# v with two adjacent keys to a partition, multiplied in 64x64 tiles; logits in the PSUM banks of the q and k transposes

## The chip, the core and the metric

The kernel runs on one NeuronCore of a Trainium2 chip. The metric is the time of one execution on the device in microseconds (us); the time before is the median of three runs. All arithmetic that the change touches is in fp32.

## The reference, cut to what matters

Chunked attention, then two layers of experts. The change lies in the attention, and only there:

```python
# q, k, v: (B, H, S, D) = (8, 8, 576, 64); chunks of 64 keys, nc = 9
scores = (q_c @ k_c^T) / 8            # per batch, head, chunk: 64 x 64
attn = exp(scores - max) ; attn = attn / (sum(attn) + 1e-9)
out = attn @ v_c                      # 64 x 64
x = out.transpose(0, 2, 1, 3).reshape(4608, 512)
# then: logits = x @ w_gate, a greedy assignment of tokens to 8 experts,
# two layers per expert, and a maximum over three products before the last one
```

## The kernel before, in words

**The work.** There are 72 chunks (8 batches of 9), 8 heads in each. A *group* g is two chunks, all heads: 128 tokens. `G` = 36 groups; a *unit* u is four groups (8 chunks), `NU` = 9 units. The fifth unit (`ORDER[4]` is None) collects the odd chunk of each of the 8 batches.

**Loads.** `load_qk` (L52) brings half of a unit's heads of q or k in one DMA of 512 KB: 128 partitions, four adjacent rows (1 KB) to a partition; in the fifth unit it is one DMA of 128 KB per chunk into 16 partitions. `load_v` (L65) is called four times per unit (`part` 0 to 3), and each call issues two DMAs of 128 KB, one on SP's queue and one on POOL's (both on SP's for unit 0; in the fifth unit four of 64 KB). A key is a partition: head 2·part lies in partitions 0 to 63 and head 2·part+1 in 64 to 127, in runs of 256 bytes. The halves that are never written are zeros from a memset (L91, L92), so that one matmul over 128 partitions gives two heads side by side. `VB` has three buffers.

**The loop over groups (L245 to L292)** is a software pipeline written out by hand; each engine takes its instructions in this order. In turn i: a small DMA `tick` (L249) that holds SP's queue back until group i-1's maxima are there; the loads of the next units; `scores(i)` (16 matmuls of 64x64, two for each pair of heads and each chunk, into the two banks of pS); `scale(i-2)` and the DMA that writes x; `smax(i)`; `att_t(i-1)`, four transposes of the exponentials into pA, and `att_c`, their copy; then `trans`/`evac` of a piece of q and of k of the next unit (transposes into one of two pT banks, copied out in halves by ACT and DVE); `ssub(i)`, `expo(i)`; `x_t(i-2)` (transposes into pY); `pv(i-1)`; the logits; `x_c(i-2)`.

**pv (L175)** issues 8 matmuls per group: 128 partitions deep, 64 columns of weights, 128 columns moving; the two chunks c go to the two halves of the 64-column tiles.

**The logits** of a finished unit are computed in two steps in a PSUM bank of their own, pL: `logit1` (L206, four matmuls in 32-column tiles, then a copy `ls` on ACT) in the turns with i mod 4 = 2, behind `pv`, and `logit2` (L223, four transposes and a reduce on DVE) in the turns with i mod 4 = 3, behind `pv` too.

**evac (L117)** of k stores the keys in their natural order: key 4i+2w+r of a chunk, where the transposes deliver r by halves of the partitions, w by transposes and i along the row.

```python
dst = QT[nm, u][s * 64:s * 64 + 64, h0:h0 + 2].rearrange("p a j (i w r) -> p a (j i) w r", w=2, r=2)[:, :, :, :, r]
```

**After the loop** (L294 to L315) the last groups and logits drain; then come routing and the experts, which wait for all logits and for x.

Of the kernel before, what the change touches and what calls it, by code (L numbers as in the profile page):

```python
# [28 lines left out]
def attention(ctx, tc, q, k, v, wg_in, xd, L, ident, consts, early, tick, mark):  # L29
# [35 lines left out]
    def load_v(u, part):  # L65

        t = VB[u % 3]
        if ORDER[u] is not None:
            b, c = chunk(u, 0)
            for s in range(2):  # L70
                (nc.gpsimd if u and s else nc.sync).dma_start(
                    t[s * 64:(s + 1) * 64, :, part, s, :],
                    bass.AP(tensor=v.tensor, offset=v.offset + (b * H + 2 * part + s) * S * D + c * 64 * D,
                            ap=[[D, 64], [64 * D, 8], [1, D]]))
            return
        for j in (2 * part, 2 * part + 1):
            b, c = chunk(u, j)
            for s in range(2):
                (nc.gpsimd if u and s else nc.sync).dma_start(
                    t[s * 64:(s + 1) * 64, j, :, s, :],  # L80
                    bass.AP(tensor=v.tensor, offset=v.offset + b * H * S * D + s * S * D + c * 64 * D,
                            ap=[[D, 64], [2 * S * D, 4], [1, D]]))

# [21 lines left out]
    def trans(nm, u, n, bank="pT"):  # L105

        mark(nm + "T")
        if n == 0:
            QT[nm, u] = P.tile([128, 4, 8, 64], F32, name=nm + "T")
        pt = PS.tile([128, 2, 2, 128], F32, name=bank, bufs=2 if bank == "pT" else 1)  # L110
        PT[nm, u, n] = pt
        for a in range(2):
            for w in range(2):
                h = 4 * (n // 2) + 2 * a + n % 2
                nc.tensor.transpose(pt[:, a, w, :], QK[nm, u][:, h, w * 128:w * 128 + 128], ident)  # L115

    def evac(nm, u, n, r, eng):  # L117
        mark(nm + "E")
        s, h0 = n % 2, 2 * (n // 2)
        src = PT[nm, u, n][r * 64:r * 64 + 64].rearrange("p a w t -> p a t w")  # L120
        dst = QT[nm, u][s * 64:s * 64 + 64, h0:h0 + 2].rearrange("p a j (i w r) -> p a (j i) w r", w=2, r=2)[:, :, :, :, r]
# [24 lines left out]
    def expo(g):  # L146
        mark("exp")
        e = P.tile([128, 8, 64], F32, name="A")
        nc.scalar.activation(e, A[g], AF.Exp, scale=0.125)
        A[g] = e  # L150

    def sums(g, st):
        mark("sums")
        if st == 0:
            R[g] = P.tile([128, 8], F32, name="sm")
            nc.vector.tensor_reduce(R[g], A[g], op=OP.add, axis=AX.X)
        elif st == 1:
            nc.vector.tensor_scalar(R[g], R[g], 1e-9, None, op0=OP.add)
        else:
            r = P.tile([128, 8], F32, name="rc")  # L160
            nc.vector.reciprocal(r, R[g])
            R[g] = r

    def att_t(g):
        mark("attT")
        PA[g] = PS.tile([128, 4, 128], F32, name="pA", bufs=1)
        for hp in range(4):
            nc.tensor.transpose(PA[g][:, hp, :], A[g][:, 2 * hp:2 * hp + 2, :], ident)  # L168

# [5 lines left out]
    def pv(g):  # L175
        mark("pv")
        u, h = divmod(g, 4)
        PX[g] = PS.tile([128, 4, 128], F32, name="pX", bufs=1)
        for hp in range(4):
            for c in range(2):  # L180
                nc.tensor.matmul(PX[g][c * 64:(c + 1) * 64, hp, :], AT[g][:, hp, c * 64:c * 64 + 64],  # L181
                                 VB[u % 3][:, 2 * h + c, hp].rearrange("p s i -> p (s i)"),
                                 start=True, stop=True)

    def scale(g):
        mark("scale")
        X[g] = P.tile([128, 8, 64], F32, name="x", bufs=3)
        nc.vector.tensor_tensor(X[g], PX[g].rearrange("p a (s i) -> p (a s) i", s=2),
                                R[g][:, :, None].to_broadcast([128, 8, 64]), op=OP.mult)
        nc.gpsimd.dma_start(xd[tokens(g) * 128:(tokens(g) + 1) * 128, :], X[g].rearrange("p h d -> p (h d)"))  # L190
# [25 lines left out]
    def logit(j, w):  # L216
        mark("logit")
        pl = PS.tile([128, 4, 128], F32, name="pT")
        for dc in range(4):
# [3 lines left out]
    def logit2(j, w0=0, w1=4):  # L223
        mark("logit2")
        pl = PS.tile([128, 4, 4, 32], F32, name="pL", bufs=1)
        for w in range(w0, w1):
# [5 lines left out]

    banks = iter(("pT", "pT", "pX", "pY", "pL", "pA", "pT", "pT"))
    for n in (0, 2):
# [76 lines left out]
    for st in (1, 2, 3):  # L311
        early(0, st)
    logit(8, 2)
    logit2(8, 0, 2)
    logit(8, 3)  # L315


# [977 lines left out]
```

## Time and profile before

| | before |
|---|---|
| median of three runs | 1206.3 us (1203.97 to 1208.42) |
| the profiled execution: its time, its span | 1207.02 us, 1205.2 us |
| PE busy | 1172.5 us (97%) |
| DVE busy | 830.5 us (69%) |
| ACT busy | 412.7 us (34%) |
| POOL busy | 317.9 us (26%) |
| mean granted TensorE clock | 0.988 of full speed |
| DMA over the span | 242.99 MB, mean 202 GB/s |
| DMA packets under 512 B, under 2 KB | 30048, 101216 |

The busy shares are means over stages with different limits; the attention takes the first 166 us or so, and there ACT and DVE are far busier than over the whole (the windows below). An fp32 matmul shows as two records on PE, so the 8 matmuls of `pv` are x16 in the trace and the 16 of `scores` are x32; transposes are one record each. A row's us is from the start of its first instruction to the end of its last; since matmuls overlap, what a group of them takes of PE is read from the start of one group to the start of the next.

### The profile page before, as it was taken

The numbers are of one execution on the slowest core, as the hardware profiler recorded it, in microseconds if no ns is written. First come the engines' busy times: TensorE is split into PE (matmuls) and PEld (weight loads), VectorE is DVE, ScalarE is ACT, GpSimd is POOL, SyncE is SP. The second block draws the span as 40 slices with busy tenths as digits, with TensorE's granted clock in tenths as the row PEclk, the third lists the DMA queues.
The fourth block names the chain that finished last, engine by engine and source line by source line (L and its number), as shares of the span: only waits on it lengthen the run. The fifth ranks groups of instructions, "written<-read, shape, count | busy, mean of one in ns | idle before, by whom it ended". The sixth has DMA issues, their size and how long they took to land.

```text
span 1205.2 us, 23575 instructions
## 1 busy us (share of the span) xinstructions
PE 1172.5 (97%) x9508; PEld 1097.6 (91%) x9508; DVE 830.5 (69%) x1660; ACT 412.7 (34%) x674; POOL 317.9 (26%) x507
## 2 busy tenths in 40 slices
PE   7999978999999999999999999999999999999998
PEld 6788856989999999989999998998998998998996
DVE  6888976788898888888843565565565565664661
ACT  5888823232333333325423113113113113113111
POOL 8433201010337463766770002002002002002002
PEclk9999989999999999999999999999999999999999
DMA  9999516264566565559834773773773763773651
GB/s 264 256 271 269 162 45 184 66 233 150 177 193 209 184 215 183 186 192 283 281 144 162 274 259 123 276 260 119 280 259 118 281 259 115 285 258 114 235 189 53
DMA packets 138828, 242.99 MB, mean 202 GB/s; under 512 B 30048, under 2 KB 101216, under 8 KB 131808
## 3 DMA queue, kind: packets, MB, share of 16 engines
q1 hardware_dynamic: 118608, 180.90, 45.9%
q0 software_dynamic: 14976, 51.13, 12.7%
q10 hardware_dynamic: 5136, 9.46, 2.1%
q8 instruction: 75, 1.23, 0.4%
q14 instruction: 33, 0.27, 0.1%
HBM read 195.05 MB, written 46.40 MB: 200 GB/s over the span
## 4 chain that ended last, share of the span: by engine, by line
PE 53%; issue 35%; DMA 4%; DVE 3%; POOL 2%; ACT 1%; POOLq 1%; SPq 1%; ACTq 0%; DVEq 0%
PE acc L1105 17%; PE acc L1050 16%; DMA vb<-in_v_dram 3%; PE pX L181 2%; PE py L1143 2%; POOL out_dram L1227 2%; PE pT L115 2%; PE po L1219 2%; PE px L1143 2%; PE pz L1143 2%; PE pS L132 1%; PE pA L168 1%; PE pxt L821 1%; PE pY L199 1%; PE rp L553 1%
## 5 line engine op out<-in xcount | busy, mean ns | idle before, releaser
L1050 PE MATMUL acc<-xhi,chunk 128*128 128x288 f32 (+2 forms) x1024 | 207.4, 302 | 2.7 <-DVE hlo L1083 2.3
L1105 PE MATMUL acc<-hhi,chunk 128*128 128x288 f32 x1024 | 209.9, 299 | 0.0
L1227 POOL DMA_INDIRECT out_dram<-ot,ia x36 | 36.3, 1008 | 519.4 <-ACT ot L1225 518.8
L1050 PEld LDWEIGHTS acc<-xhi,chunk 128*128 128x128 f32 x1024 | 161.9, 189 | 3.8 <-DVE hlo L1083 2.7
L1105 PEld LDWEIGHTS acc<-hhi,chunk 128*128 128x128 f32 x1024 | 163.0, 188 | 0.3
L1105 PE MATMUL acc<-hlo,chunk 128*128 128x288 f32 x512 | 150.9, 295 | 0.0
L1219 PE MATMUL po<-chunk,h 128*128 128x512 f32 x648 | 149.3, 390 | 0.0
L1219 PEld LDWEIGHTS po<-chunk,h 128*128 128x128 f32 x648 | 121.5, 188 | 24.8
L1050 PE MATMUL acc<-xlo,chunk 128*128 128x288 f32 (+2 forms) x512 | 143.9, 296 | 0.0
L1143 PE MATMUL px<-xb,wa 128*128 128x384 f32 x648 | 130.0, 335 | 0.7 <-ACT ys L1112 0.7
L1143 PE MATMUL py<-xt,wb 128*128 128x384 f32 x648 | 129.9, 335 | 0.0
L1143 PEld LDWEIGHTS px<-xb,wa 128*128 128x128 f32 x648 | 113.9, 188 | 1.4 <-ACT ys L1112 1.0
L1143 PEld LDWEIGHTS py<-xt,wb 128*128 128x128 f32 x648 | 114.0, 188 | 0.5
L1164 ACT CAST h<-best 128x384 fp32r<-128x384 f32 x72 | 37.0, 513 | 198.1 <-DVE best L1162 121.3
L1105 PEld LDWEIGHTS acc<-hlo,chunk 128*128 128x128 f32 x512 | 96.2, 188 | 0.0
L1050 PEld LDWEIGHTS acc<-xlo,chunk 128*128 128x128 f32 x512 | 94.1, 189 | 0.0
L768 DVE TENSOR_TENSOR chunk<-raw,chunk 128x1024 fp32r<-128x1024 f32 x67 | 84.8, 1271 | 6.5 <-ACT chunk L761 5.7
L1074 ACT ACTIVATE hhi<-acc 128x576 fp32r<-128x576 f32 (+1 forms) x66 | 41.8, 637 | 137.2 <-PE acc L1050 135.3
L798 POOL DMA_INDIRECT xg<-xd,idx x40 | 43.3, 1082 | 169.2 <-DVE ohe L688 89.7
L1179 ACT COPY tmp<-px 128x384 f32<-128x384 f32 x54 | 25.8, 478 | 146.3 <-PE px L1143 146.3
L761 ACT CAST chunk<-raw 128x1024 fp32r<-128x1024 f32 x67 | 69.7, 1047 | 7.8 <-ACT ys L1112 6.4
L1083 DVE SCALAR_TENSOR_TENSOR hlo<-acc,hhi 128x576 fp32r<-128x576 f32 (+1 forms) x66 | 48.2, 735 | 30.9 <-ACT hhi L1074 30.5
(222 smaller groups left out, 2058.5 us busy)
## 6 DMA issues: line engine op xcount, KB each, us to landing
wb<-wdb SPq DMA_DIRECT2D x54, 1024.0 KB
wa<-wda SPq DMA_DIRECT2D x54, 768.0 KB
raw<-in_moe_w_dram SPq DMA_DIRECT2D x64, 512.0 KB
xd<-x POOLq DMA_DIRECT2D x36, 256.0 KB, 4.8
yd<-ys ACTq DMA_DIRECT2D x32, 288.0 KB
wdb<-pair POOLq DMA_DIRECT2D x18, 512.0 KB, 4.7
yraw<-yd SPq DMA_DIRECT2D x12, 768.0 KB
ink<-in_k_dram SPq DMA_DIRECT2D x16, 512.0 KB
```

The source lines that it names most:

```text
L761: nc.scalar.copy(hi, raw)
L768: nc.vector.tensor_tensor(lo, raw, hi.bitcast(F32), op=OP.subtract)
L798: nc.gpsimd.indirect_dma_start(out=g, out_offset=None, in_=xd[:, :], in_offset=bass.IndirectOffsetOnAxis(ap=rt.idx[r][:, t:t + 1], axis=0))
L1050: nc.tensor.matmul(acc[:, hf, :tk.stop - tk.start], w[a][:, dc, o:o + 128], x[:, dc, tk], start=n == 0, stop=n == 11)
L1074: nc.scalar.activation(hv, src, AF.Relu)
L1083: nc.vector.scalar_tensor_tensor(lv, src, 0.0, hv.bitcast(F32), op0=OP.max, op1=OP.subtract)
L1105: nc.tensor.matmul(acc[:, hf, :288], w[a][:, f, :], x[:, f, tk], start=n == 0, stop=n == 23)
L1143: nc.tensor.matmul(dst, w[:, dc, o, a], XO[x][:, c, dc], start=start and n == 0, stop=stop and n == 5, skip_group_check=True)
L1164: nc.scalar.copy(hpart(g, i, j)[0], M)
L1179: nc.scalar.copy(U[g, 1], XB[g])
L1219: nc.tensor.matmul(PO[t], h[:, x, t % 6 * 128:t % 6 * 128 + 128], w[a][:, f % 2], start=f == 0 and n == 0, stop=f == 5 and n == 2)
L1227: st = nc.gpsimd.indirect_dma_start(out=out, out_offset=bass.IndirectOffsetOnAxis(ap=ia[:, t:t + 1], axis=0), in_=ot, in_offset=None)
```

## The change

What it does:

- **v.** A partition holds two adjacent keys of a head, 512 bytes in a run. `load_v`'s DMAs have the same 128 KB, now 32 partitions of 8 runs of 512 bytes. Heads are placed by 4i+2s+x: i picks the half of the partitions, s the 32 partitions in it. The whole of each `VB` buffer is set to zero by one memset, so the loads come behind it.
- **pv.** 16 matmuls per group in place of 8: 64 partitions deep, 64 columns of weights, 128 moving; two of them (r = 0 and 1, the even and the odd keys) add up in one place. The halves i write to two banks; PX is now [128, 2, 512].
- **The exponentials** are stored with even and odd keys apart, so `expo` writes, `sums` reads and `scale` reads other patterns of as many elements.
- **k.** `evac` of k reads and writes in the transposes' own order (r, w, j, i), and `scores` reads its moving operand in the order r, i, w: the innermost step is 128 elements, where it was one.
- **Logits.** pL is given up. `logit1` and `logit2` take pT banks; `logit1` stands behind `scores` and `smax` in the turns with i mod 4 = 3, `logit2` there in those with i mod 4 = 0. The last `logit(8, 3)` takes pY. Five of the eight first transposes move to other banks.

```diff
     def load_v(u, part):
-        t = VB[u % 3]
-        if ORDER[u] is not None:
-            b, c = chunk(u, 0)
-            for s in range(2):
+        t, (x, i) = VB[u % 3], divmod(part, 2)
+        for s in range(2):
+            rows, head = slice(64 * i + 32 * s, 64 * i + 32 * s + 32), 4 * i + 2 * s + x
+            for e in range(1 if ORDER[u] is not None else 2):
+                b, c = chunk(u, e)
+                dst, n, step = (t[rows, :, x, s], 8, 64 * D) if ORDER[u] is not None else (t[rows, e::2, x, s], 4, 2 * H * S * D)
                 (nc.gpsimd if u and s else nc.sync).dma_start(
-                    t[s * 64:(s + 1) * 64, :, part, s, :],
-                    bass.AP(tensor=v.tensor, offset=v.offset + (b * H + 2 * part + s) * S * D + c * 64 * D,
-                            ap=[[D, 64], [64 * D, 8], [1, D]]))
...
+                    dst.rearrange("p j r d -> p j (r d)"),
+                    bass.AP(tensor=v.tensor, offset=v.offset + (b * H + head) * S * D + c * 64 * D,
+                            ap=[[2 * D, 32], [step, n], [1, 2 * D]]))
...
-    VB = [C.tile([128, 8, 4, 2, 64], F32, name="vb%d" % i) for i in range(3)]
+    VB = [C.tile([128, 8, 2, 2, 2, 64], F32, name="vb%d" % i) for i in range(3)]
     for t, eng in ((VB[0], nc.vector), (VB[1], nc.gpsimd), (VB[2], nc.gpsimd)):
-        eng.memset(t[0:64, :, :, 1, :], 0.0)
-        eng.memset(t[64:128, :, :, 0, :], 0.0)
+        eng.memset(t, 0.0)
...
+        if nm == "k":
+            src = PT[nm, u, n][r * 64:r * 64 + 64]
+            dst = QT[nm, u][s * 64:s * 64 + 64, h0:h0 + 2].rearrange("p a j (x t) -> p a (j x t)", x=2).rearrange(
+                "p a (r w t) -> p a r w t", r=2, w=2)[:, :, r]
...
     def scores(g):
+        keys = QT["k", u].rearrange("p a j x -> p a (j x)").rearrange("p a (r w j i) -> p a j r i w", r=2, w=2, j=8)
...
-                    nc.tensor.matmul(PSS[g][to, hp, s], QT["q", u][o, hp, 2 * h + c], QT["k", u][o, hp, 2 * h + c],
+                    nc.tensor.matmul(PSS[g][to, hp, s], QT["q", u][o, hp, 2 * h + c], keys[o, hp, 2 * h + c],
...
     def expo(g):
-        e = P.tile([128, 8, 64], F32, name="A")
-        nc.scalar.activation(e, A[g], AF.Exp, scale=0.125)
+        e = P.tile([128, 4, 4, 32], F32, name="A")
+        nc.scalar.activation(e.rearrange("t n a p -> t a n p"), A[g].rearrange("t (a s) (r p) -> t a (s r) p", s=2, r=2),
+                             AF.Exp, scale=0.125)
...
     def pv(g):
-        PX[g] = PS.tile([128, 4, 128], F32, name="pX", bufs=1)
-        for hp in range(4):
-            for c in range(2):
-                nc.tensor.matmul(PX[g][c * 64:(c + 1) * 64, hp, :], AT[g][:, hp, c * 64:c * 64 + 64],
-                                 VB[u % 3][:, 2 * h + c, hp].rearrange("p s i -> p (s i)"),
-                                 start=True, stop=True)
+        PX[g] = PS.tile([128, 2, 512], F32, name="pX", bufs=1)
+        for x in range(2):
+            for r in range(2):
+                for c in range(2):
+                    for i in range(2):
+                        o = slice(i * 64, i * 64 + 64)
+                        nc.tensor.matmul(PX[g][c * 64:(c + 1) * 64, i, :256].rearrange("p (s x d) -> p x s d", s=2, x=2)[:, x],
+                                         AT[g][o, 2 * x + r, c * 64:c * 64 + 64], VB[u % 3][o, 2 * h + c, x, :, r],
+                                         start=r == 0, stop=r == 1, tile_position=(i * 64, c * 64))
...
     def logit1(j, w0=0, w1=4):
-        pl = PS.tile([128, 512], F32, name="pL", bufs=1)
+        pl = PS.tile([128, 512], F32, name="pT")
...
             smax(i)
+        if i >= 7 and i % 4 == 3:
+            logit1(i // 4 - 1)
+        if i >= 8 and i % 4 == 0:
+            logit2(i // 4 - 2)
...
-        if i >= 7 and (i - 4) % 4 == 3 and i < G - 1:
-            logit2((i - 4) // 4)
-        if i >= 6 and (i - 3) % 4 == 3 and i < G:
-            logit1((i - 3) // 4)
```

How the instructions stand. First **PE**, from the end of turn 6 to the beginning of turn 8 (the names are tiles: pX is pv's result, pS scores, pA the transposed exponentials, pT the transposes of q and k, pY those of x, pL the logits; x4 and so on count equal instructions). Before:

```order
L181 MATMUL pX<-vb_94,AT 64x128 x8
L211 MATMUL pL<-xT,wg 32x512 x4
L132 MATMUL pS<-kT,qT 64x64 x16
L168 MATMUL pA<-ident,A 128x128 x4
L115 MATMUL pT<-ident,inq 128x128 x4
L115 MATMUL pT<-ident,ink 128x128 x4
L199 MATMUL pY<-ident,x 128x128 x4
L181 MATMUL pX<-vb_94,AT 64x128 x8
L227 MATMUL pL<-ident,ls 128x128 x4
L132 MATMUL pS<-kT,qT 64x64 x16
```

Now:

```order
L188 MATMUL pX<-vb_94,AT 64x2x64 x16
L134 MATMUL pS<-kT,qT 64x64 x16
L219 MATMUL pT<-xT,wg 32x512 x4
L172 MATMUL pA<-ident,A 128x128 x4
L111 MATMUL pT<-ident,inq 128x128 x4
L111 MATMUL pT<-ident,ink 128x128 x4
L207 MATMUL pY<-ident,x 128x128 x4
L188 MATMUL pX<-vb_94,AT 64x2x64 x16
L134 MATMUL pS<-kT,qT 64x64 x16
L235 MATMUL pT<-ident,ls 128x128 x4
L172 MATMUL pA<-ident,A 128x128 x4
```

Both logit steps have moved from between pv and scores to between scores and the transposes of the exponentials: logit1 from the end of turn 6 into turn 7, logit2 from the end of turn 7 into turn 8.

**ACT** in the same turn 7, before:

```order
L122 COPY qT<-pT 64x512
L214 COPY ls<-pL 128x512
L204 COPY xT<-pY 128x4x128
L173 COPY AT<-pA 128x512
L122 COPY qT<-pT 64x512
L122 COPY kT<-pT 64x512
L149 ACTIVATE A<-A_793 128x512
```

Now:

```order
L123 COPY qT<-pT 64x512
L212 COPY xT<-pY 128x4x128
L222 COPY ls<-pT 128x512
L177 COPY AT<-pA 128x512
L123 COPY qT<-pT 64x512
L123 COPY kT<-pT 64x2x256
L151 ACTIVATE A<-A_837 128x4x4x32
```

The copy `ls` has changed places with the copy of x's transposes and stands directly ahead of AT; what it reads is produced later on PE.

**SP**'s queue around the first loads of v, before:

```order
L60 DMA inq<-in_q_dram 128x4x256
L71 DMA vb_93<-in_v_dram 64x8x64 x8
L60 DMA ink<-in_k_dram 128x4x256
L60 DMA inq<-in_q_dram 128x4x256
L60 DMA ink<-in_k_dram 128x4x256
```

Now:

```order
L60 DMA inq<-in_q_dram 128x4x256
L73 DMA vb_93<-in_v_dram 32x8x128 x8
L60 DMA ink<-in_k_dram 128x4x256
L60 DMA inq<-in_q_dram 128x4x256
L60 DMA ink<-in_k_dram 128x4x256
```

The DMAs are as many and in the same places; each of v's has half the partitions and twice the run.

## Rows read from the trace of the kernel before

**Rows 1.** Windows: stretch, its us, busy time by engine, granted clock, DMA share, GB/s.

```profile
core 0: us, PE busy (x) PEld busy (x) DVE busy (x) ACT busy (x) POOL busy (x), PEclk, DMA share, GB/s
...
22.00:26.00 4.00, 3.53 (x22) 3.23 (x24) 1.56 (x4) 2.14 (x4) 3.91 (x15) 0.57 1.13 279
...
56.00:60.00 4.00, 4.00 (x51) 3.77 (x48) 2.57 (x4) 1.36 (x3) 2.55 (x4) 0.57 1.10 216
60.00:100.00 40.00, 40.00 (x674) 32.92 (x673) 34.93 (x72) 35.31 (x62) 13.97 (x23) 1.00 1.10 273
```

**Rows 2.** Timeline of PE, 0 to 60 us: start, us, line, operation [idle <-releaser].

```profile
19.66 0.44 PE L181 MATMUL pX<-vb,AT 128*64 128x128 f32 x4 [1.78 <-DMA vb<-in_v_dram]
...
22.47 1.09 PE L115 MATMUL pT<-ident,inq 128*128 128x128 f32 x4 [1.16 <-DMA inq<-in_q_dram]
...
55.74 0.44 PE L181 MATMUL pX<-vb,AT 128*64 128x128 f32 x4 [1.78 <-DMA vb<-in_v_dram]
```

**Rows 3.** Timeline of PE, 117 to 126 us: one turn and the next.

```profile
117.19 1.09 PE L181 MATMUL pX<-vb,AT 128*64 128x128 f32 x16
...
118.21 0.70 PE L132 MATMUL pS<-kT,qT 64*64 64x64 f32 x32
...
118.84 0.66 PE L168 MATMUL pA<-ident,A 128*128 128x128 f32 x4
...
119.33 0.60 PE L115 MATMUL pT<-ident,inq 128*128 128x128 f32 x4
...
119.77 0.60 PE L115 MATMUL pT<-ident,ink 128*128 128x128 f32 x4
...
120.21 0.60 PE L199 MATMUL pY<-ident,x 128*128 128x128 f32 x4
...
120.74 1.09 PE L181 MATMUL pX<-vb,AT 128*64 128x128 f32 x16
...
121.76 0.70 PE L132 MATMUL pS<-kT,qT 64*64 64x64 f32 x32
```

**Rows 4.** Timeline of PE, 118.20 to 118.35 us: the seam of pv and scores.

```profile
118.01 0.28 PE L181 MATMUL pX<-vb,AT 128*64 128x128 f32 x2
118.21 0.35 PE L132 MATMUL pS<-kT,qT 64*64 64x64 f32 x8
```

**Rows 5.** DMA view, 3 to 9 us: q, k; 128 partitions, 1 KB runs.

```profile
DMA packets 2592, 2.07 MB, mean 344 GB/s; under 512 B 591, under 2 KB 2592, under 8 KB 2592
```

**Rows 6.** DMA view, 13 to 17 us: v; 64 partitions, 256 B runs.

```profile
DMA packets 3041, 0.78 MB, mean 195 GB/s; under 512 B 3029, under 2 KB 3040, under 8 KB 3040
```

**Rows 7.** Waits of DVE, 60 to 143 us: total us, times, longest.

```profile
DVE kT L122 <- ACT kT L122: 5.3, 11, 1.5
```

**Rows 8.** The chain that ended last: one logit1 on PE, start and us.

```profile
125.38 1.00 PE pL L211 x8
```

**Rows 9.** Timeline, 142 to 147 us: last turn of a unit.

```profile
142.16 0.69 PE L132 MATMUL pS<-kT,qT 64*64 64x64 f32 x32
...
142.34 0.59 ACT L214 COPY ls<-pL 128x512 f32<-128x512 f32 x1
...
143.54 0.58 ACT L173 COPY AT<-pA 128x512 f32<-128x512 f32 x1
...
145.97 0.62 ACT L122 COPY qT<-pT 64x512 f32<-64x512 f32 x1
...
146.30 0.80 PE L132 MATMUL pS<-kT,qT 64*64 64x64 f32 x32
```

**Rows 10.** Tile vb: loads on SP, last memset on DVE, ns.

```profile
L71 SPq DMA_DIRECT2D vb<-in_v_dram x36: 601/633/2452, 5.1 to 140.1; - x36
...
L92 DVE MEMSET vb<- x1: 1765/1765/1765, 3.6 to 3.6; 64x2048 f32 x1
```

**Rows 11.** DMA view, 50 to 54 us: q, k; 16 partitions, 1 KB runs.

```profile
DMA packets 496, 0.76 MB, mean 189 GB/s; under 512 B 160, under 2 KB 368, under 8 KB 496
```

More of the change, by code (lines that the diff above doesn't have):

```diff
@@ L65, in load_v @@
     def load_v(u, part):
-        t = VB[u % 3]
-        if ORDER[u] is not None:
-            b, c = chunk(u, 0)
-            for s in range(2):
-                (nc.gpsimd if u and s else nc.sync).dma_start(
-                    t[s * 64:(s + 1) * 64, :, part, s, :],
-                    bass.AP(tensor=v.tensor, offset=v.offset + (b * H + 2 * part + s) * S * D + c * 64 * D,
-                            ap=[[D, 64], [64 * D, 8], [1, D]]))
[L75 to L82, printed above, removed]
+        t, (x, i) = VB[u % 3], divmod(part, 2)
[4 more added lines that the diff above has]
+                dst, n, step = (t[rows, :, x, s], 8, 64 * D) if ORDER[u] is not None else (t[rows, e::2, x, s], 4, 2 * H * S * D)
+                (nc.gpsimd if u and s else nc.sync).dma_start(
+                    dst.rearrange("p j r d -> p j (r d)"),
+                    bass.AP(tensor=v.tensor, offset=v.offset + (b * H + head) * S * D + c * 64 * D,
+                            ap=[[2 * D, 32], [step, n], [1, 2 * D]]))
     for h in (0, 4):
@@ L109, in trans @@
             QT[nm, u] = P.tile([128, 4, 8, 64], F32, name=nm + "T")
-        pt = PS.tile([128, 2, 2, 128], F32, name=bank, bufs=2 if bank == "pT" else 1)
+        if isinstance(bank, str):
+            pt = PS.tile([128, 2, 2, 128], F32, name=bank, bufs=2 if bank == "pT" else 1)
+        else:
+            pt = bank.rearrange("p (a w t) -> p a w t", a=2, w=2)
         PT[nm, u, n] = pt
@@ L120, in evac @@
         src = PT[nm, u, n][r * 64:r * 64 + 64].rearrange("p a w t -> p a t w")
-        dst = QT[nm, u][s * 64:s * 64 + 64, h0:h0 + 2].rearrange("p a j (i w r) -> p a (j i) w r", w=2, r=2)[:, :, :, :, r]
+        if nm == "k":
+            src = PT[nm, u, n][r * 64:r * 64 + 64]
+            dst = QT[nm, u][s * 64:s * 64 + 64, h0:h0 + 2].rearrange("p a j (x t) -> p a (j x t)", x=2).rearrange(
+                "p a (r w t) -> p a r w t", r=2, w=2)[:, :, r]
+        else:
+            dst = QT[nm, u][s * 64:s * 64 + 64, h0:h0 + 2].rearrange("p a j (i w r) -> p a (j i) w r", w=2, r=2)[:, :, :, :, r]
         (nc.vector.tensor_copy if eng else nc.scalar.copy)(dst, src)
@@ L155, in sums @@
             R[g] = P.tile([128, 8], F32, name="sm")
-            nc.vector.tensor_reduce(R[g], A[g], op=OP.add, axis=AX.X)
+            nc.vector.tensor_reduce(R[g].rearrange("t (a s) -> t a s", s=2), A[g].rearrange("t (s r) a p -> t a s r p", r=2),
+                                    op=OP.add, axis=AX.XY)
         elif st == 1:
@@ L166, in att_t @@
         PA[g] = PS.tile([128, 4, 128], F32, name="pA", bufs=1)
-        for hp in range(4):
-            nc.tensor.transpose(PA[g][:, hp, :], A[g][:, 2 * hp:2 * hp + 2, :], ident)
+        for n in range(4):
+            nc.tensor.transpose(PA[g][:, n, :], A[g].rearrange("t n a p -> t n (a p)")[:, n], ident)
     def att_c(g):
@@ L177, in pv @@
         u, h = divmod(g, 4)
-        PX[g] = PS.tile([128, 4, 128], F32, name="pX", bufs=1)
-        for hp in range(4):
-            for c in range(2):
-                nc.tensor.matmul(PX[g][c * 64:(c + 1) * 64, hp, :], AT[g][:, hp, c * 64:c * 64 + 64],
-                                 VB[u % 3][:, 2 * h + c, hp].rearrange("p s i -> p (s i)"),
-                                 start=True, stop=True)
+        PX[g] = PS.tile([128, 2, 512], F32, name="pX", bufs=1)
[7 more added lines that the diff above has]
+                                         start=r == 0, stop=r == 1, tile_position=(i * 64, c * 64))
     def scale(g):
@@ L187, in scale @@
         X[g] = P.tile([128, 8, 64], F32, name="x", bufs=3)
-        nc.vector.tensor_tensor(X[g], PX[g].rearrange("p a (s i) -> p (a s) i", s=2),
-                                R[g][:, :, None].to_broadcast([128, 8, 64]), op=OP.mult)
+        nc.vector.tensor_tensor(X[g].rearrange("p (i h) d -> p i h d", i=2),
+                                PX[g][:, :, :256].rearrange("p i (h d) -> p i h d", d=64),
+                                R[g].rearrange("p (i h) -> p i h", i=2)[:, :, :, None].to_broadcast([128, 2, 4, 64]), op=OP.mult)
         nc.gpsimd.dma_start(xd[tokens(g) * 128:(tokens(g) + 1) * 128, :], X[g].rearrange("p h d -> p (h d)"))
@@ L214, in logit1, with logit @@
         nc.scalar.copy(LS[j][:, t], pl[:, t])
-    def logit(j, w):
+    def logit(j, w, bank):
         mark("logit")
-        pl = PS.tile([128, 4, 128], F32, name="pT")
+        pl = PS.tile([128, 4, 128], F32, name=bank, bufs=2 if bank == "pT" else 1)
         for dc in range(4):
@@ L224, in logit2 @@
         mark("logit2")
-        pl = PS.tile([128, 4, 4, 32], F32, name="pL", bufs=1)
+        pl = PS.tile([128, 4, 4, 32], F32, name="pT")
         for w in range(w0, w1):
@@ L231, in logit2 @@
                                 pl[:, w0:w1, :, :8].rearrange("p w a e -> p w e a"), op=OP.add, axis=AX.X)
-    banks = iter(("pT", "pT", "pX", "pY", "pL", "pA", "pT", "pT"))
+    px = PS.tile([128, 2, 512], F32, name="pX", bufs=1)
+    banks = iter(("pT", "pT", "pY", px[:, 0], px[:, 1], "pA", "pT", "pT"))
     for n in (0, 2):
@@ L312, in attention @@
         early(0, st)
-    logit(8, 2)
+    logit(8, 2, "pT")
     logit2(8, 0, 2)
-    logit(8, 3)
+    logit(8, 3, "pY")
 class Clock:
```

## The prediction

> **What bounds the kernel now.** All of the change lies in the attention, so I read the windows first: from 60 to 100 us PE is busy in all of 40.00 us, DVE in 34.93, ACT in 35.31, and the DMA engines move 273 GB/s with a share above 1 [rows 1]. PE sets the pace there, with DVE and ACT close behind. In two earlier stretches, 22 to 26 us and 56 to 60 us, the granted clock is 0.57 [rows 1]: most of each ran at the lower of TensorE's two levels. The timeline shows what came before each: PE stood 1.78 us for v (until 19.66) and 1.16 us for q (until 22.47), and 1.78 us for v of unit 2 (until 55.74) [rows 2]. So there are two regimes: up to about 56 us transfers hold PE up at three places, after that PE holds itself up.
>
> The steady turn is in rows 3. From start to start: pv 1.02, scores 0.63, transposes of the exponentials 0.49, of q 0.44, of k 0.44, of x 0.53, in all 3.55 us. Four transposes cost 0.44 behind other transposes; 0.49 and 0.53 stand where PE goes over to another tile shape. The seam of pv and scores shows it alone: the last pair of pv starts at 118.01 and scores at 118.21, 0.20 apart [rows 4], where pv's eight pairs are 0.82/7 = 0.12 apart (117.19 to 118.01). So a change of shape costs about 0.09 us ahead of it and, by 0.49 against 0.44, 0.05 behind it: **0.14 us**, three times in a turn.
>
> For the loads: alone on the queues, q and k (128 partitions, 1 KB runs) move at 344 GB/s [rows 5], v of unit 0 (64 partitions, 256 B runs) at 195 GB/s [rows 6]. DVE waits mostly on ACT's half of k, 5.3 us in 83 [rows 7], so it has little slack.
>
> **The change, part by part.**
>
> *pv.* Twice the matmuls, half the depth, as many columns. What matters is how many run side by side: before two at a time (eight pairs), now tiles of the shape that scores has. Scores takes 32 records in 0.63 us [rows 3], seams included; at two at a time it would need sixteen steps of about 0.055 (half a pair's 0.12, for half the columns), 0.88. So four run at a time, and pv stays at eight steps of 0.12: nothing gained or lost. Bounds: 0 if as scores; +0.9 us per group if only two ran at a time; rows 3 lie at the first end.
>
> *Seams.* pv and scores now have one shape: 36 groups x 0.14 = **-5.0 us**. logit2, a transpose, had two seams more than a turn without it; behind scores and ahead of transposes it has none of its own: 7 x 0.14 = **-1.0 us**. logit1 has two in either place.
>
> *logit1's new place.* It is 1.00 us of PE [rows 8], now ahead of the exponentials' transposes in the last turn of a unit. Now, AT starts 1.38 us behind scores there, the last copy of q 2.43 us later, and ends at 146.59, 4.43 us behind scores; the next scores, which need that q from their second half on, start 4.14 us behind and already take 0.80 in place of 0.70 [rows 9]. With logit1 ahead AT starts about 1.0 us later, so q is there at 5.4; PE, at 3.40 + 1.00 = 4.40 for the turn, wants it at 4.75. I take a new wait of 0.6 us (beyond the 0.1 of now) at 7 unit ends: **+4.2 us**. Bounds 0 (ACT makes the time up) and +7. The pT banks themselves add no wait that I can price: logit1 takes the bank that k has left, and ls is copied out while the exponentials and q are transposed (0.93 us by rows 3 against a copy of 0.59).
>
> *v of unit 0.* Eight DMAs of 128 KB are 1.05 MB, 5.4 us at 195 GB/s. Runs of 512 B lie between the two rows: 256 B at 195 GB/s are 21 ns on each of 16 engines, 1 KB at 344 are 48, so linearly 30 ns, 273 GB/s, 3.8 us. Everything behind it in SP's queue comes 1.6 us earlier, which the waits until 19.66 and 22.47 can use in full: **-1.6 us**. Bounds: 0 if the run's length is not what limits it, -2.4 at 344 GB/s. The low clock at 22 us I leave as it is, since a good part of the idle time before it stays.
>
> *v of unit 2.* The wait until 55.74 is for a load on SP's queue issued at the time of the loads of the fifth unit. With half as many runs to go through I take it as gone (-1.8), and with it the low clock behind it, 4 us x 0.43 = 1.7: **-3.5 us**. Bounds 0 and -3.5.
>
> *At nothing, with cover.* The memset in one piece needs what the two did (2 x 1.77 us, from 1.4 us on), ending near 5.0; the first load of v is issued at 5.1 [rows 10] and its data queue behind q and k. Without cover 0.3. expo, sums, scale and k's copies keep their element counts; ACT and DVE have the slack of rows 1, and without it each 0.05 per turn would be 1.8. The last logit(8, 3) changes banks beside an idle queue.
>
> *scores' moving operand* steps 128 elements at its innermost. No row has such a read in fp32. Bounds: 0, and twice the 0.49 us that scores takes without seams, +17.6 in 36 groups. I take 0 in the sum, as every matmul row of rows 3 runs at its column count's pace; the other end is a rival.
>
> Sum: -5.0 - 1.0 + 4.2 - 1.6 - 3.5 = **-6.9 us**. The profiled execution took 1207.0 us, 0.7 above the median of 1206.3; from the median the forecast is 1199.4, rounded **1199.5 us**.
>
> **The rivals.**
>
> *Loads bound by where they land, 1204.5.* In 50 to 54 us 1 KB runs also go at 189 GB/s, into 16 partitions [rows 11]: there the run's length did not help. If v's 195 GB/s are due to the 64 partitions, 32 will do no better, both load terms vanish and the PE terms alone remain: -1.8. Against it: rows 11 has POOL's other traffic in it. [...]
>
> *Scores slowed by its strided read, 1213.* If a read that jumps 512 bytes at each column takes twice as long, scores costs +17.6; the seams give 6.0 back, the wait at unit ends is then hidden (PE comes later), the load terms stay: 17.6 - 6.0 - 5.1 = +6.5. It decides from scores at about 0.63 + 0.19 = 0.82 us per group (6.9/36). For it: the step is that of no other operand. Against it: fp32 columns go by slowly already, 128 in 0.11 us. [...]
>
> *DVE takes over, 1203.* With the seams gone PE needs 15.0 us per unit (4 x 3.40 + 1.00 + 0.44). If the reduce over two axes or the read of two banks costs DVE a tenth more, it needs as long as PE does now; then only the load terms remain, halved by demand that stays close behind them: -3.5.
>
> **How the numbers follow.** About 0.5% of this time, 6 us, is what a measurement tells from no change: faster is below 1200.3, slower above 1212.3. Chances: the forecast 0.46 (its own range 1195 to 1203: v at 344 GB/s and the first low clock gone at one end, half of the second load term and the wait at unit ends at the other), loads bound by partitions 0.24, strided read 0.17, DVE 0.13. Faster: 0.7 of the first and a tenth of the second and the fourth, 0.36, and I round up for waits that may vanish together: 0.38. Slower: 0.6 of the third and some of pv's other bound, 0.13. Same: 0.49. The range 1193 to 1211 leaves out a strided read that costs the full double and a clean sweep of every wait.
>
> **What would show it.** In the profile after: from pv's start to scores' start about 0.95 and no step of 0.20 between them; scores still 0.63 (0.8 or more: the third rival); a wait of scores on qT once per unit; v of unit 0 at about 270 GB/s (195: the second rival); no wait on vb near 50 us and a granted clock of 1.00 where 0.57 stood; PE busy throughout from 60 us on (DVE waiting for nothing: the fourth). The forecast is wrong if the turn is longer than 3.55 us or if the attention ends less than 4 us earlier.

## The result, and the profile after

| | before | after |
|---|---|---|
| median, us | 1205.58 (6 runs, 1203.31 to 1208.42) | 1214.63 (6 runs, 1212.65 to 1215.87) |
| profiled execution, us | 1207.02 | 1212.65 |
| its span, us | 1205.2 | 1210.9 |
| scores of the last group begin, us | 156.50 | 164.87 |
| attention's last matmul begins, us | 165.45 | 174.78 |

After over before is 1.0069, 95% interval 1.005 to 1.0089: 9 us slower, where 7 us faster was forecast and 1211 was the end of the range. The attention carries it: in the profiles its last group starts 8.4 us later and its last matmul 9.3 us, and the distance is still 8.7 us at 200 us. It shrinks only where the profiled execution of before lost 2.9 us, to a wait for DVE and a stretch of half clock at 517 to 524 us that the other does not have.

The windows of the changed kernel, as in [rows 1]:

```profile
core 0: us, PE busy (x) PEld busy (x) DVE busy (x) ACT busy (x) POOL busy (x), PEclk, DMA share, GB/s
22.00:26.00 4.00, 3.52 (x81) 3.29 (x82) 2.86 (x7) 2.81 (x5) 3.75 (x15) 1.00 1.12 308
56.00:60.00 4.00, 3.82 (x98) 3.40 (x88) 3.73 (x8) 3.71 (x7) 1.48 (x3) 1.00 1.16 230
60.00:100.00 40.00, 36.13 (x709) 31.51 (x712) 30.94 (x62) 30.82 (x55) 13.20 (x24) 0.96 0.95 238
...
15.20:18.60 3.40, 3.40 (x43) 3.28 (x44) 2.57 (x4) 2.17 (x5) 2.99 (x11) 0.51 1.15 240
46.00:49.30 3.30, 3.30 (x17) 1.92 (x10) 1.69 (x3) 0.99 (x2) 0.00 (x0) 0.50 0.51 124
63.10:66.40 3.30, 3.23 (x18) 3.11 (x18) 1.88 (x3) 1.20 (x2) 0.60 (x1) 0.50 1.17 162
```

Both low stretches of [rows 1] now run at full clock (the forecast had this of the second and left the first as it was); but three others are at half. PE, busy in all of 40 us before, now stands for 3.87 of them. The two traces grant 1.00 or 0.50 and nothing between: the 0.57 of [rows 1] are 0.50 from 22.3 to 25.7 and from 56.4 to 59.8 us.

The timeline of PE says where (start, us, line, operation, idle time before it and what ended it):

```profile
18.83 1.10 PE L188 MATMUL pX<-vb,AT 64*64 64x128 f32 x32
...
22.48 0.63 PE L111 MATMUL pT<-ident,inq 128*128 128x128 f32 x4 [1.40 <-DMA inq<-in_q_dram]
...
30.13 0.49 PE L134 MATMUL pS<-kT,qT 64*64 64x64 f32 x12 [0.43 <-issue]
...
35.93 0.67 PE L188 MATMUL pX<-vb,AT 64*64 64x128 f32 x16
38.09 0.74 PE L188 MATMUL pX<-vb,AT 64*64 64x128 f32 x14 [1.50 <-issue]
...
42.19 0.72 PE L134 MATMUL pS<-kT,qT 64*64 64x64 f32 x28
45.42 0.35 PE L134 MATMUL pS<-kT,qT 64*64 64x64 f32 x4 [2.52 <-issue]
...
59.11 0.71 PE L134 MATMUL pS<-kT,qT 64*64 64x64 f32 x27
63.17 0.48 PE L134 MATMUL pS<-kT,qT 64*64 64x64 f32 x5 [3.35 <-issue]
```

The waits for v of [rows 2] are gone. In their place PE stops in the middle of a group of matmuls, with operands and bank long there, and the releaser is "issue": nothing that the profile shows. Count PE's records (matmuls, weight loads, semaphore instructions) from the first on: these four, and a fifth of 0.73 us at 101.81, come ahead of number 705, 961, 1217, 1729 and 3265, counting from 0. The distances are 256, 256, 512 and 1536, all whole multiples of 256. And the queues of the profile's DMA part (packets, MB, share of 16 engines) hold the other half:

```profile
q8 instruction: 79, 1.29, 0.5%
```

1.29 MB in 79 packets are 16 KB each, and 20,349 records of PE over 79 are 258: one packet per 256 instructions of PE. Before, it was 75 packets (1.23 MB) for 19,229 records. The packets' times in the trace fit: the stalls that end at 30.13, 38.09, 45.42, 63.17 and 101.81 end 1.34 to 1.65 us after the end of such a packet. The reading of these: **PE had run out of instructions.** pv has 16 matmuls and 16 weight loads a turn more than before, so a block lasts less long (6.1 us in the mean from 66 to 130 us, where it was 7.4); the experiments ask whether that, or the loads that the packet meets on its way, makes the next block late.

The profile of the kernel before has the same sign once, ahead of its own record 3265, 1.4 us after the end of a packet:

```profile
110.81 0.34 PE L132 MATMUL pS<-kT,qT 64*64 64x64 f32 x5 [0.30 <-issue]
```

The seam, from PE's timeline (a turn and a unit's end), against [rows 3, 4, 9]:

```profile
55.63 0.73 PE L134 MATMUL pS<-kT,qT 64*64 64x64 f32 x32
56.29 0.66 PE L172 MATMUL pA<-ident,A 128*128 128x128 f32 x4
...
58.19 1.10 PE L188 MATMUL pX<-vb,AT 64*64 64x128 f32 x32
59.11 0.71 PE L134 MATMUL pS<-kT,qT 64*64 64x64 f32 x27
...
121.95 0.57 PE L134 MATMUL pS<-kT,qT 64*64 64x64 f32 x18
122.91 0.50 PE L134 MATMUL pS<-kT,qT 64*64 64x64 f32 x14 [0.39 <-ACT qT L123]
```

pv to scores is 0.92 (was 1.02), scores 0.66 (was 0.63), the turn 3.48 (was 3.55). The new wait for q at a unit's end is there. And v alone on the queues, 13 to 17 us, against [rows 6]:

```profile
DMA packets 1616, 0.80 MB, mean 201 GB/s; under 512 B 97, under 2 KB 1616, under 8 KB 1616
```

### The profile page after: what moved, and what is told of

It is laid out like the page before. It is cut to its first block, busy times and chain, and to the rows that moved or that the text cites. A ratio compares the mean times of both kernels' runs of the same rounds, so it can differ in the third digit from the quotient of the medians.

```text
span 1210.9 us, 24697 instructions
## 1 busy us (share of the span) xinstructions
PE 1172.7 (97%) x10084; PEld 1101.6 (91%) x10084; DVE 827.3 (68%) x1659; ACT 412.1 (34%) x674; POOL 311.2 (26%) x505
## 3 DMA queue, kind: packets, MB, share of 16 engines
q8 instruction: 79, 1.29, 0.5%
## 4 chain that ended last, share of the span: by engine, by line
PE 49%; issue 37%; DVE 4%; ACT 4%; POOL 2%; DMA 2%; POOLq 1%; SPq 0%; ACTq 0%; DVEq 0%
PE acc L1114 17%; PE acc L1059 16%; PE py L1152 2%; POOL out_dram L1236 2%; PE px L1152 2%; PE pz L1152 2%; PE pxt L830 1%; PE pX L188 1%; PE po L1228 1%; PE pS L134 1%; ACT qT L123 1%; PE pA L172 1%; PE pT L111 1%; DMA vb<-in_v_dram 1%; PE rp L562 1%
```

## The experiments

The theory: late blocks of instructions. Its rivals: v's new loads, the logits' new place, PE's own extra work. All times below are medians, with the ratio to the kernel before (run on the same chip as each, 1206 to 1207 us) and its 95% interval; the ratio is made from all runs and not from the two medians. Each kernel has one traced execution, so the times of waits are those of one execution. Single rows are from the waits of PE between 24 and 160 us (line, releaser, us in total, times, longest).

**e1: the logits put back behind pv.**

```
-        if i >= 7 and i % 4 == 3:
-            logit1(i // 4 - 1)
-        if i >= 8 and i % 4 == 0:
-            logit2(i // 4 - 2)
...
+        if i >= 7 and (i - 4) % 4 == 3 and i < G - 1:
+            logit2((i - 4) // 4)
+        if i >= 6 and (i - 3) % 4 == 3 and i < G:
+            logit1((i - 3) // 4)
```

> The changed kernel with the two logit stages put back behind pv (turns 4u+2 and 4u+3), in the banks of the transposes as the change has them. Fetch theory: four fifths of the loss is TensorE running out of instructions between 24 and 66 us (its stalls stand at instruction 705, 961, 1217, 1729 and 3265 of its own count, each a whole number of 256s apart, and add up to 8.5 us), because pv now issues 32 instructions instead of 16; so the stalls stay, at other times perhaps, and only the unit ends come back, 0.3 to 0.6 us at each of seven: 1210 to 1213 us. Place theory: the logit's new place holds the scores up at every unit's end and pushes the loads behind it: 6 to 9 us come back, 1205 to 1208 us, and the stalls with them.

1213.96 us (1.0062, 1.004 to 1.0084), a little above the fetch theory's range and far from the place theory's: the place is not the cause.

```profile
PE pS L134 <- issue: 5.6, 2, 3.2
PE pT L219 <- DVE kT L123: 2.6, 6, 0.5
PE pT L235 <- DVE kT L123: 1.9, 7, 0.5
```

The late blocks stay (two, 2.43 and 3.15 us, at records 705 and 1729), and the waits at units' ends only change their name: in the old place the logits wait for their bank, which DVE's copy of k still holds. Away from late blocks a unit takes 16.67 us here (scores at 106.77 and 123.44), against 16.17 in the changed kernel.

**e2: the kernel before with only the logits moved.**

```
+        if i >= 7 and i % 4 == 3:
+            logit1(i // 4 - 1)
+        if i >= 8 and i % 4 == 0:
+            logit2(i // 4 - 2)
...
-        pl = PS.tile([128, 512], F32, name="pL", bufs=1)
+        pl = PS.tile([128, 512], F32, name="pT")
```

> The kernel before with only the logit stages moved to their new place and into the banks of the transposes; loads, scores and pv as before. Fetch theory: no stall of TensorE without a releaser between 24 and 66 us, unit ends 0.3 to 0.6 us longer: 2 to 4 us over the kernel before. Place theory: 7 to 9 us over it. A third way: nothing at all, if the seams saved at logit2 pay for the wait.

1208.08 us (1.0012, 0.9999 to 1.0024), 1.6 us over the kernel before, which the interval does not tell from nothing: less than both theories expected. In the trace a unit takes 16.28 us (scores at 114.48 and 130.76) against 15.85, the 0.3 to 0.6 that the fetch theory had, and one block is 0.52 us late, where it had none.

**e3: the kernel before with pv in 16 matmuls of half the columns.**

```
-                nc.tensor.matmul(PX[g][c * 64:(c + 1) * 64, hp, :], AT[g][:, hp, c * 64:c * 64 + 64],
-                                 VB[u % 3][:, 2 * h + c, hp].rearrange("p s i -> p (s i)"),
-                                 start=True, stop=True)
+                for s in range(2):
+                    nc.tensor.matmul(PX[g][c * 64:(c + 1) * 64, hp, s * 64:s * 64 + 64], AT[g][:, hp, c * 64:c * 64 + 64],
+                                     VB[u % 3][:, 2 * h + c, hp, s], start=True, stop=True)
```

> The kernel before with each of pv's eight matmuls issued as two of half the columns, so pv has 32 instructions instead of 16 and everything else, the loads too, is as before. Fetch theory: TensorE stalls without a releaser at whole numbers of 256 of its instructions between 20 and 70 us, 3 to 10 us in sum, on top of 36 times 0.1 to 0.3 us for the longer pv (4 to 11 us): 7 to 18 us over the kernel before. Load theory (the new form of v's loads starves the fetch or the data, whatever TensorE issues): no such stall, 4 to 11 us over the kernel before.

1211.7 us (1.0038, 1.002 to 1.0056).

```profile
PE pS L132 <- issue: 2.7, 1, 2.7
```

One late block, at record 1729, in a kernel that has old loads, old logits and, without the edit, no block that is later than 0.30 us. The stall of 2.7 us is somewhat under the 3 to 10 of the fetch theory, and the sum of 5.2 us is under its 7; by the time alone the load theory (4 to 11) would hold, but it allowed no such stall. The rest is the longer pv: a unit takes 16.19 us (scores at 117.89 and 134.08) against 15.85, some 3 us in nine.

**e4: the changed kernel with half of pv.**

```
-            for r in range(2):
+            for r in range(1):
...
-                                         start=r == 0, stop=r == 1, tile_position=(i * 64, c * 64))
+                                         start=True, stop=True, tile_position=(i * 64, c * 64))
```

> The changed kernel with half of pv left out (the products of the odd keys): 8 matmuls and 8 weight loads a turn, as many instructions as before the change, while v's loads keep their new form. Fetch theory: no stall over 0.3 us at a whole number of 256 instructions between 24 and 66 us, and the turn is then bounded by VectorE at about 3.5 us: 8 to 14 us under the changed kernel. Load theory: the stalls at about 30, 38, 45 and 63 us stay, 5 to 8 us in sum, and no more than 3 to 5 us come off.

1200.97 us (0.9957, 0.9939 to 0.9975), 13.6 us under the changed kernel.

```profile
PE pT L111 <- issue: 1.3, 1, 1.3
```

One late block of 1.29 us where none was expected, against 8.5 us in five: the new loads alone do not make those. The run also has less to multiply, so its time says less than its stalls.

**e5 and e6: v's loads crossed with the rest of the change.** e5 is the changed kernel with v's old loads, e6 the kernel before with the new ones and the memset in one piece that goes with them; the core of e6:

```
+                dst, n, step = (t[rows, :, x, s], 8, 64 * D) if ORDER[u] is not None else (t[rows, e::2, x, s], 4, 2 * H * S * D)
...
-                            ap=[[D, 64], [64 * D, 8], [1, D]]))
+                            ap=[[2 * D, 32], [step, n], [1, 2 * D]]))
```

> The changed kernel with v loaded as before (64 partitions, runs of 256 B, the fifth unit's too) into the same tile, which leaves the keys in the wrong order and changes nothing else. Count theory (pv's 16 more instructions a turn use up a block of 256 before the next has come): stalls of TensorE at its instruction 193 plus a multiple of 256 between 24 and 66 us stay, 3 to 8 us in sum: 1210 to 1216 us. Load theory (v's new loads delay the blocks): those stalls are gone or under 1 us in sum: 1203 to 1207 us.

> The kernel before with v loaded as the change does (32 partitions, runs of 512 B) into the same tile, keys in the wrong order, all else as before. Count theory: at most 0.5 us of stalls at such block ends, and what pv(0) waited for v (1.78 us) is shorter: 1202 to 1206 us. Load theory: 3 to 8 us of such stalls, 1209 to 1214 us.

e5: 1213.75 us (1.0056, 1.0037 to 1.0076). e6: 1202.49 us (0.9964, 0.994 to 0.9988). The waits of PE in e5:

```profile
PE pS L140 <- issue: 7.2, 2, 4.0
```

and in e6:

```profile
PE pT L108 <- issue: 3.2, 1, 3.2
```

This square clears the loads. In the kernel before the new loads are 4 us faster, in the changed one they change nothing that can be measured; under either load the rest of the change (pv, the logits' place, the order of keys) costs 7 to 12 us, of which e2 and e3 have the logits' place and pv's count alone at 1.6 and 5.2. But e6 has one late block, of 3.16 us at 57.00, where the count theory allowed 0.5 and the load theory had 3 to 8: a block can be late at the old count too, when its packet starts 7.1 us after the block before it was entered.

**e7 and e8: v loaded once, in the changed kernel and in the one before.** pv then reads the first unit's buffer throughout; the loads:

```
         if tr:
-            load_v(u, n)
+            pass
```

> The changed kernel with v of the first unit loaded once and used for all units (a third of the bytes loaded after 20 us is left out). If the DMA queues' load is what makes the blocks of instructions late: no stall at a block end over 0.3 us, the time from block entered to packet started falls from 2 to 6 us to under 1.5 us, and 9 to 13 us come off: 1201 to 1206 us. If TensorE outruns the fetch even on free queues: half of the stalls or more stay, 1207 to 1212 us.

> The kernel before with the same loads of v left out. It has no stall at a block end to lose; its two waits for v (1.78 us each, with the low clock after one) go for the later one: 1 to 4 us off, 1202 to 1206 us. Fetch theory: so the two kernels differ here by -3 to +2 us, where with all loads the changed one is 9 us longer. Place theory (logits' new place): the difference stays at 4 us or more.

e7: 1207.93 us (1.0011, 0.9988 to 1.0033), single executions from 1200 to 1213. e8: 1201.03 us (0.9951, 0.9937 to 0.9966). Of e7:

```profile
PE pA L172 <- issue: 2.5, 1, 2.5
```

The packets start sooner (2.3 us after the block's entry in the mean, against 4.4) and 2.5 us of late blocks are left of 8.5; e8 has none. So fewer bytes to load helped here, but did not cure it. The two medians are 6.9 us apart, where -3 to +2 was expected; the place theory's sign, 4 us or more, is there, though e1 and e2 speak against the place. e7's profiled execution, at 1205.8 us, is on the fast side of a wide spread; what its slower ones do was not traced, so where these 6.9 us go is not shown.

**e9, e10: the unit with 16-partition loads taken eighth, after and before.**

```
-    ORDER = [0, 1, 2, 3, None, 4, 5, 6, 7]
+    ORDER = [0, 1, 2, 3, 4, 5, 6, None, 7]
```

> The changed kernel with the unit whose q and k go to 16 partitions a load taken as the eighth instead of the fifth, so its loads are issued at about 110 to 125 us instead of 43 to 64. Fetch theory: the two longest stalls (2.52 us at 45.42, 3.35 us at 63.17) come while these loads fill the queues; without them blocks arrive 1 to 3 us earlier and 3 to 7 us come off: 1207 to 1212 us. Against it: a block lasts TensorE 5.5 to 6.3 us here and the other loads alone keep the queues as full: 1213 to 1216 us.

> The kernel before with the same unit taken as the eighth. It has no stall at a block end; its wait for v at 55.74 us (1.78 us, with 1.7 us of low clock behind it) stands behind these loads on POOL's queue: 2 to 4 us off, 1203 to 1205 us. If the wait only moves to the eighth unit: 1206 to 1208 us.

e9: 1216.01 us (1.0072, 1.0048 to 1.0097). e10: 1204.04 us (0.9972, 0.9956 to 0.9989). Of e9:

```profile
PE pA L172 <- issue: 4.6, 1, 4.6
PE pS L134 <- issue: 3.8, 2, 2.4
PE pX L188 <- issue: 3.7, 2, 2.2
```

and of e10:

```profile
PE pS L132 <- issue: 3.8, 1, 3.8
```

The longest late block moves with these loads, to 115.09 us in e9 and to 111.22 in e10: the longest delays come with them, at either instruction count. Moving them saves nothing in the changed kernel (e9 missed the 1207 to 1212 of the fetch theory) and 2 us in the one before, whose wait for v at 55.74 goes. That wait was not for POOL's queue, as these expectations and e11's have it: in the trace of before it ends with the load of v that SP issued at 41.70, whose last part landed at 55.60.

**e11, e12: v ahead of q and k in each turn of the kernel before; the same with the late unit.**

```
+        if tr:
+            load_v(u, n)
         for nm, h in LOADS[i] if i < 4 else [("kq"[n % 2], n // 2 * 4)]:
...
-        if tr:
-            load_v(u, n)
```

> The kernel before with each turn's load of v issued ahead of its loads of q and k. The wait of pv(8) for v of the third unit (1.78 us at 55.74) goes, as that load no longer stands behind five of k on POOL's queue: 2 to 4 us off, 1203 to 1205 us. Rival: q or k of the next unit is late instead, and nothing is gained: 1206 to 1209 us.

> Both edits on the kernel before (the unit with short loads taken eighth, v issued ahead of q and k). If they remove the same wait: the same 2 to 4 us off, 1202 to 1205 us. If each removes a wait of its own: 1200 to 1202 us.

e11: 1206.84 us (0.9991, 0.9974 to 1.0009); q is late instead. e12: 1204.61 us (0.9982, 0.9966 to 0.9997), as e10 alone. The wait that e11 has in place of the one for v is the first of these, of transposes of q at 68.66 us (they do not read x; the releaser's name is inferred). The second is the wait for q at the start, 1.16 us in [rows 2]:

```profile
PE pT L115 <- DMA xd<-x: 2.4, 1, 2.4
PE pT L115 <- DMA inq<-in_q_dram: 1.8, 1, 1.8
```

**e13, e14, e15: loads taken from POOL's queue to SP's** (v's alone in the changed kernel; all; all in the kernel before).

```
-                (nc.gpsimd if u and s else nc.sync).dma_start(
+                nc.sync.dma_start(
...
-            (nc.gpsimd if j >= 4 else nc.sync).dma_start(
+            nc.sync.dma_start(
```

> The changed kernel with all of v's loads issued by SP instead of half by POOL. Queue theory (a block waits behind the 4 KB packets of POOL's queue): packet starts 1 to 2 us sooner after a block is entered, the stalls between 24 and 66 us shrink from 7.8 us to under 4: 1206 to 1211 us. Bytes theory (it waits behind whatever is on the way): stalls as before, 1212 to 1217 us. A third way: SP issues too late, and waits for v or for q and k come on top: 1215 to 1225 us.

> The changed kernel with all loads of q, k and v on SP; POOL's queue then holds the stores of x alone. Queue theory: stalls at block ends under 2 us in sum, 1203 to 1209 us. Bytes theory: 1212 to 1217 us. Third way (SP too late): 1215 to 1225 us.

> The kernel before with all loads of q, k and v on SP. It has no stall at a block end to lose: within 2 us of the kernel before if SP keeps up, and the wait for v at 55.74 us may go (another 2 to 3 us off: 1202 to 1206 us). If SP is too late: 1208 to 1220 us.

e13: 1209.64 us (1.0029, 1.0014 to 1.0044). e14: 1207.36 us (1.001, 0.9995 to 1.0025). e15: 1203.92 us (0.9981, 0.9962 to 1.0). Of e14:

```profile
PE pS L134 <- ACT qT L123: 3.4, 8, 0.7
PE pT L219 <- issue: 1.9, 1, 1.9
PE pS L134 <- issue: 1.7, 2, 1.5
```

The bytes are the same and SP keeps up. The blocks' packets start sooner (3.1 and 2.4 us after entry, against 4.4), the late blocks fall to 5.3 and 3.3 us, somewhat more than was expected to be left, and 5 and 7 us come off. Nor were the queues emptier: between 24 and 66 us they moved 264 and 257 GB/s, against 224 in the changed kernel. So it is not bytes alone: in these kernels the packets of instructions started 2.0 us later (4.4 against 2.4) with part of the loads issued by POOL (after) than with all issued by SP (e14). One difference of form is in the traces: between 24 and 130 us of the changed kernel POOL's queue has packets of 4 KB, 0.19 us each in the median, SP's has runs of 512 B and 1 KB, 0.04 and 0.05 us. Whether that is the reason was not tried.

**e16: e14 with the logits back; e17: e15 with the unit of 16-partition loads eighth.**

> The changed kernel with all loads on SP and the two logit stages back behind pv. If the logits' place costs what it did in the kernel before (1.6 us): 1204.5 to 1206.5 us. If the difference to the kernel before is all late blocks (3.3 us of stalls are left): no change, 1206.5 to 1208.5 us.

> The kernel before with all loads on SP and the unit with 16-partition loads taken as the eighth. If the two edits each remove their own waits: 1200.5 to 1203 us, under both kernels. If the fifth unit's loads only carry their late block along, as with POOL's queue (3.83 us at 111.22 there): 1203 to 1206 us.

e16: 1209.6 us (1.002, 1.0005 to 1.0036): 2 us above e14, with intervals that overlap; the logits wait for their bank there (as in e1), and a late block of 2.33 us appears. Neither way held. e17: **1201.71 us (0.9951, 0.9934 to 0.9968), faster than both kernels**, without a late block; its waits:

```profile
PE pX L181 <- ACT AT L173: 1.2, 4, 0.4
PE pT L115 <- DMA vb<-in_v_dram: 0.6, 1, 0.6
PE pS L132 <- ACT qT L122: 0.3, 1, 0.3
```

All runs together, one traced execution each. A block's entry is PE's record 193 or a whole number of 256s behind it; a late block is a stall of over 0.3 us ahead of it (the one of before at 110.81 is just under that); delay is from the entry of a block to the start of the next packet of 16 KB:

| kernel | late blocks, 24 to 130 us | their sum, us | delay, 24 to 66 us, mean | a block lasts, 66 to 130 us, mean |
|---|---|---|---|---|
| before | 0 | 0 | 3.6 | 7.4 |
| after | 5 | 8.5 | 4.4 | 6.1 |
| e1 | 2 | 5.6 | 4.2 | 6.2 |
| e2 | 1 | 0.5 | 3.8 | 7.6 |
| e3 | 1 | 2.7 | 3.6 | 6.1 |
| e4 | 1 | 1.3 | 4.5 | 7.6 |
| e5 | 5 | 8.9 | 4.3 | 6.3 |
| e6 | 1 | 3.2 | 4.1 | 7.4 |
| e7 | 1 | 2.5 | 2.3 | 6.3 |
| e8 | 0 | 0 | 2.4 | 7.5 |
| e9 | 5 | 10.7 | 3.0 | 7.2 |
| e10 | 1 | 3.8 | 2.9 | 8.3 |
| e11 | 0 | 0 | 3.7 | 7.4 |
| e12 | 2 | 3.2 | 3.7 | 7.8 |
| e13 | 4 | 5.3 | 3.1 | 6.2 |
| e14 | 2 | 3.3 | 2.4 | 6.4 |
| e15 | 1 | 0.8 | 1.3 | 7.6 |
| e16 | 3 | 4.4 | 3.0 | 6.6 |
| e17 | 0 | 0 | 1.7 | 7.6 |

The last two columns say how near a kernel is to late blocks. A packet takes 1.3 us and PE goes on 1.3 to 2.0 us after its end, so a block is there some 2.8 us after the packet's start: 3.6 + 2.8 = 6.4 us against the 7.4 that a block lasts before, 4.4 + 2.8 = 7.2 against 6.1 after. In the mean the margin was 1 us, and the change took more than that. The means do not give the sums: a single packet's delay decides, so e13 and e16 have late blocks although their means leave a margin, and e3, whose mean leaves none, has only one.

## Why the prediction was wrong

**The step that failed** is "nothing gained or lost" for pv. By PE's time that was right: 32 records in 0.92 us, where 16 took 1.02; that four tiles ran at a time is the prediction's estimate from [rows 3]. But the term counted columns and left the 16 more matmuls and 16 more weight loads a turn free, as instructions. That was five late blocks, 8.5 us in the profiled execution, and a half clock behind two of them (46.0 to 49.3 and 63.1 to 66.4 us). No rival had it. The forecast's own sign of being wrong came true by it: the turn is shorter (3.48 us), as forecast, but the attention ends 9.3 us later. Which rows could have told it: the stall of 0.30 us at 110.81 with the releaser "issue"; beside it the profile of before lists an instruction queue with 75 packets, and its DMA shares are above 1 [rows 1].

Point by point:

- *Seams, -5.0 and -1.0.* Right in kind, half in size: 0.10 a turn at pv and scores instead of 0.14, 0.03 of it given back by scores; 0.07 x 36 is -2.5 us.
- *logit1's place, +4.2.* Right in kind, and in sum larger than the seams: away from late blocks a unit takes 16.17 us (scores at 121.95 and 138.12) against 15.85 before (114.59 and 130.44), seams included. At seven unit ends that is 7 x 0.32 = +2.2 us, where the same terms gave 7 x (0.6 - 0.14 - 4 x 0.14) = -0.7.
- *v of unit 0, -1.6.* The rate did not rise: 201 GB/s against 195, as packets of 512 B took 47 ns in the median where those of 256 B took 28, and e6 has 202 GB/s with the same loads. The second rival had this outcome; that the partitions are its cause was not shown, as no run changes them without the run's length. Nor did what stands behind v come earlier: the q for which PE waits next landed at 22.34 us in both profiles, and its transposes start at 22.47 and 22.48. That pv(0) no longer waits is lost again in that wait. scores(4) does start 1.67 us earlier, at 28.31 us instead of 29.98, about the number forecast, but by luck: the half clock of 22.3 to 25.7 us, which the forecast left as it is, is gone, and the one of 15.2 to 18.6 us lies ahead of the wait for q and costs nothing. Half clock begins between 20 and 25 us in seven of the ten traces with v's old loads and in one of the nine with the new ones; why is open. scores(4) before, and after:

```profile
29.98 0.56 PE L132 MATMUL pS<-kT,qT 64*64 64x64 f32 x18
...
28.31 0.57 PE L134 MATMUL pS<-kT,qT 64*64 64x64 f32 x18
```

- *v of unit 2, -3.5.* The wait went (-1.8), in e6 too, where the loads alone are new and the half clock behind it is gone as well. In the changed kernel half clock came back behind the late blocks.
- *scores' strided read, taken at 0.* 0.03 us a group (0.66 against 0.63), 1 us in all, and far from the rival's double, which no run shows.
- *DVE.* Its waits for ACT's half of k rose, from 5.3 us in [rows 7] to 9.4 in the same stretch; it does not set the pace, as no wait of PE over 0.3 us from 60 to 160 us ends with DVE.

```profile
DVE kT L123 <- ACT kT L123: 9.4, 11, 1.5
```

The sum as measured, up to the last scores: late blocks 8.5, unit ends 2.2, the wait for v of unit 2 -1.8, half clock even (two stretches of 3.4 us that cost time in either profile): 8.9 us, where the two profiles are 8.4 apart.

What is shown: PE stops at whole blocks of 256 of its instructions, 35 times between 24 and 130 us, in 15 of the 19 kernels, each time until 1.3 to 2.0 us after the end of a 16 KB packet, and at no other place in that stretch does it stand over 0.15 us without a releaser. More instructions in pv bring such stops to kernels whose loads are unchanged (one in e3, five in e5), fewer leave one of 1.3 us (e4); loads on SP instead of POOL shorten them at the same bytes (e13, e14). What is argued: that a block is asked for when the one before it is entered. Of the 264 blocks entered and left between 24 and 130 us in the 19 traces, 260 have exactly one packet start in them; twice a packet started up to 0.6 us ahead of the entry; the shortest delay is 0.06 us. What stays open: the parts do not add up (pv's count alone 5.2 us, the logits' place alone 1.6, the loads alone -4.2, which makes 2.6 where the change costs 9), and why the count alone makes one late block and the whole change five is not shown, as the new order of keys was never run by itself. Open too are why the packets of instructions start later where POOL issues loads, why e7 varies by 13 us, and whether the order of PE's instructions could hide the late blocks, which was not tried.

## What to carry to other kernels

In the attention of this kernel, with a DMA share of 0.98 from 26 to 66 us (1.11 before), there was a second budget beside columns: instructions of PE per microsecond. So when an edit splits matmuls into smaller tiles, it is worth counting records per turn: 256 divided by them, times the length of a turn, estimates how long a block lasts, to be set against the time from its entry until PE goes on with the next. Here a block lasted 7.4 us before against 6.4 needed, and 6.1 after against 7.2. A wait with the releaser "issue" in the middle of a group of matmuls was the sign; its distance of whole 256s of records from the next such wait, and the end of a 16 KB packet 1.3 to 2.0 us before it, confirmed it. Moving loads from POOL's queue to SP's was the remedy that helped here: 7 us in the changed kernel (e14), which still is no faster than the kernel before.

## What the runs showed of the hardware

- PE's instructions come in packets of 16 KB, one per 256 (79 packets for 20,349 records, after), on a queue that the profile lists with those of the data; with v's loads left out after the first unit they start sooner (4.4 to 2.3 us, e7). A packet started up to 7.6 us after the block before was entered (e10), and PE stood for up to 4.6 us (e9). The changed kernel has 8.5 us of such stalls between 24 and 130 us.
- The same bytes issued by SP instead of POOL let these packets start 2 us sooner (4.4 to 2.4 us, e14; 3.6 to 1.3 us, e15).
- A matmul in fp32 whose moving operand steps 512 bytes at each column took 0.66 us a group (after) instead of 0.63 (before).
- Twice the run's length, 512 B for 256, into half the partitions left the rate at 201 (after) and 202 (e6) against 195 GB/s (before), 13 to 17 us.
